# Sketched attention and a two-expert router on one core: due times of one batch's loads, the place of the last query sketches, and three steps moved between engines

## The chip, the cores and the metric

The program runs on one core of a Trainium2 chip. The metric is the device time of one execution in microseconds (us). The core has five engines that run at the same time, each through its own list of instructions in order: TensorE (PE; its weight loads are listed as PEld), VectorE (DVE), ScalarE (ACT), GpSimd (POOL) and SyncE (SP). SP here only issues DMA transfers; ACT and POOL issue some as well.

## The reference, cut to what matters

Four batches of four heads, 1088 tokens of 32 values each. `phi` is a feature map: two small projections (`S1`, `S2`, 8 rows each) and the outer product of their results, 64 features a token.

```python
q_p, k_p = phi(q), phi(k)
kv  = einsum('bhsf,bhsd->bhfd', k_p, v)
z   = sum(k_p, axis=2)
x   = (q_p @ kv) / (q_p . z + 1e-6)        # heads joined: (4352, 128)
logits = x @ w_gate + log1p(exp(x @ w_noise)) * noise
# the two largest of 8 logits choose two experts, softmax over the two
out = sum over the two of  weight * relu(x @ w1[e]) @ w2[e]     # 128 -> 1024 -> 128
```

## The kernel before, in words

**Stages.** For each batch, keys and queries are turned so that a token's values lie on the partitions (DVE, `turned`, L585 and L587), sketched by products with the two projections (`features`: PE L601, then a copy `lo` L319, a sum `ab` L608 and a product `phk` or `phq` L622), and the values are copied into `vaug` (ACT, L319 and L639). PE sums keys times values (L659) into `kvp`; two copies `kvT`, a product with the gate weights (`fold`, L680) and two copies `kvw` make the small matrix from which `queries` gets numerators, denominators and gate logits: PE turns `phq` (L704), a copy `pT`, PE L715, then on DVE `den` (L744, L745), `lh` and `lg`. `router` turns logits into the two experts, the gates and each token's row in its expert's list, and POOL sends the rows to DRAM by indirect DMA (`xs`, L796), one instruction for 128 rows. The tokens are routed in five waves: wave 0 is tiles 0 to 3 of batch 0, wave 1 is the rest of batch 0, waves 2 to 4 are batches 1 to 3.

**Expert blocks.** `block` takes 128 or 256 rows of one expert: `bT` (the rows, turned), PE L1081 with `w1`, a relu `h` (L1089, on ACT), PE L1096 with `w2` into `acc`, a copy `y`, and an indirect DMA of `y` to `pairs`. There are 48 blocks, with 4 + 4 + 8 products of 128 columns for each 128 rows, every product two records in the trace. The first four blocks (`DIRECT`) don't wait for rows in DRAM: a one-hot matrix `o` (L1026, four pieces of 128x128, on DVE) picks the rows out of `x` on PE (L1032, into `turn`). Blocks 4 to 7 fetch their rows through POOL; the later ones through SP, and DVE turns those (`bT<-xb`, L1071).

**What sets the order.** Nothing is ordered by the hardware at run time except by waits. A planner (`Plan`) takes jobs with an engine or a choice of engines (`EV` is ACT or DVE), a cost, a priority (lower goes first) and dependencies, and simulates the engines: of the jobs that can start within 0.3 us of the earliest one it takes the one of the lowest priority number. The order that comes out is each engine's list of instructions. A load's end is planned from its size at 320 GB/s, one transfer after the other, plus a `margin`; the margin is not a wait on the chip, it only tells the planner from when on a job that reads the data may be put into an engine's list. Where PE would be idle before 28 us of planned time, `idle` fills the gap with products of zeros (L1401, into `hp`), as many as fit the planned gap, some of them tied to steps of the router.

**Names that the change touches.** `load_kq` and `load_v` load keys, queries and values (SP; for batch 0, values by SP and ACT in turn); all copies L639 and L319 of batch 1's `vaug` are ACT's. `constants` has the load of ACT's function table (L511, priority 3; the first value loads have priority 1 and are issued by ACT too). `kvT` is one tile, its two halves copied by ACT or DVE as the plan has it. `rest_of_queries` sketches the last five query tiles of batch 0 (one of 64 tokens, four of 128); before, both pieces wait for the gather of block 0 and write a `bank`. In wave 0 of `router`, POOL makes `a` (L856), `row` (L857) and their sum (L858), and then three steps on `sp` (L861 to L863); DVE's `noisy` (L875) waits for these. After it on DVE come `top`, `pick`, `first`, `mk`, `gm`, `pos` and block 0's `o`.

**Buffers.** Of `bank` there are 3 in PSUM, of `acc`, `hp` 2 and of `turn` 1; of `vld` 1 and of `kq` 2.

Of the kernel before, what the change touches and what calls it, by code (L numbers as in the profile page):

```python
# [13 lines left out]
ALU = mybir.AluOpType  # L14
# [23 lines left out]
class Plan:  # L38
# [17 lines left out]
    def new(self, tag):  # L56
        return Buf(tag)
# [117 lines left out]
def kernel(  # L175
# [15 lines left out]
    P = nc.NUM_PARTITIONS  # L191
    B, H, S, DH = q.shape
    R = S1.shape[0]
# [9 lines left out]
    C = 8  # L203
    HB = 64
    YW = DH + 1 + 2 * E
# [22 lines left out]
    V, A, G, T, Y = nc.vector, nc.scalar, nc.gpsimd, nc.tensor, nc.sync  # L228
# [4 lines left out]
    def add(engines, cost, emit, **kw):  # L233

        if hold and engines in ("DVE", "PE"):
            kw["after"] = tuple(kw.get("after", ())) + tuple(hold)
        elif hold and engines == EV:
            engines = "ACT"
        return plan.add(engines, cost, emit, **kw)
# [3 lines left out]
    def tag(name, bufs, shape, dtype=F32, space=pool):  # L243
        plan.tag(name, bufs, lambda: space.tile(list(shape), dtype, name=name, tag=name, bufs=bufs))
# [16 lines left out]
    tag("qT", 1, [P, S])  # L261
    tag("lo", 2, [P, 4, 2 * R * H])
    tag("ab", 2, [P, 4 * H, 2, R])
    tag("kvT", 1, [P, 2, 2, R * R])
    tag("pT", 2, [P, 512])
    tag("den", 2, [P, 2 * H])
    tag("lh", 2, [P, 2 * H, 2 * E])
# [25 lines left out]
    def vec(n):  # L293
        return 0.155 + 0.00104 * n

    def act(n):
        return 0.155 + 0.00086 * n
# [7 lines left out]
    def mm(n):  # L305
        return max(0.205, 0.016 + 0.00162 * n)
# [6 lines left out]
    def either(n):  # L313
        return {"ACT": act(n), "DVE": vec(n)}
# [3 lines left out]
    def copy(e, o, i):  # L318
        paces.append(A.copy(o, i) if e == "ACT" else V.tensor_copy(o, i))  # L319
# [32 lines left out]
    def load_kq(b, which, prio):  # L352
        t = new("kq")
        {"k": klds, "q": qlds}[which][b] = t
        src = {"k": k, "q": q}[which]
        dma("SP", lambda: t.t[:], lambda: pairs_of(src[b]), (), [t], prio, size=557e3,
                  margin=MARGIN if b > 1 else 1.0 if b else QLATE if which == "q" else KLATE)

    def load_v(b, prio, queues=("SP",)):
        t = new("vld")  # L360
        vlds[b] = t
        src = v[b].rearrange("h (t n) d -> t h n d", n=TN)
        for l in range(4):
            dma(queues[l % len(queues)], lambda l=l: t.t[32 * l:32 * l + 32, :, 0:C, :].rearrange("p h c d -> p h (c d)"),
                lambda l=l: src[:, :, C * l:C * l + C, :].rearrange("t h c d -> t h (c d)"),
                (), [(t, l)], prio, size=131e3, issue=1.2, margin=MARGIN if b > 1 else 1.0 if b else VLATE)
        for l in range(2):
            dma(queues[l % len(queues)], lambda l=l: t.t[32 * l:32 * l + 32, :, C, :], lambda l=l: src[:, :, 32 + l, :],
                (), [(t, 4 + l)], prio, size=16e3, issue=0.6)

    w1s = const.tile([P, E, F], F32, name="w1s")
    w2s = const.tile([P, E, FJ, D], F32, name="w2s")
# [62 lines left out]
    def constants():  # L435
# [72 lines left out]
        add("DVE", 0.3, lambda e: (V.tensor_copy(starts[:, 0, :], base[:]), V.memset(over[:], -1.0)),  # L508
            r=["base"], w=[("starts", 0), "over"], prio=45)

        add("ACT", TABLE, lambda e: A.preload_act_table_set("natural_log_exp_and_others"), w=["tables"], prio=3)  # L511

    began = []

# [73 lines left out]
                            s[:, 0:P * C].rearrange("p (l c d) -> p c l d", l=4, d=DH)[:, c0:c1, :, :])  # L588
        add("DVE", vec(128 * (c1 - c0) if c0 < C else 64), emit, r=[src], w=[(dst, t) for t in range(c0, c1)], prio=prio)

    def features(jobs, prio, after=(), first=None):

        ps = new("bank")
        n = len(jobs)
        rows = slice(0, HB if jobs[0][1] == C else P)
        W = 2 * R * H

        def emit(e):
            for i, (xT, t, _) in enumerate(jobs):
                lhsT = xT.t[:, P * t:min(P * t + P, S)]  # L600
                T.matmul(ps.t[rows, 2 * W * i:2 * W * i + 2 * W], lhsT=lhsT,  # L601
                         rhs=sk[:].rearrange("p c h x -> p (c h x)"), start=True, stop=True)
        last = add("PE", n * mm(128), emit, lat=0.15, r=["sk"] + [(xT, t) for xT, t, _ in jobs],
                   w=[ps], prio=prio if first is None else first, touch=[dst for _, _, dst in jobs], after=after)
        lo, ab = new("lo"), new("ab")
        x4 = lambda: ps.t[rows, 0:2 * W * n].rearrange("p (i c y) -> p i c y", i=n, c=2)
        add(EV, either(W * n), lambda e: copy(e, lo.t[rows, 0:n, :], x4()[:, :, 1, :]), r=[ps], w=[lo], prio=prio)
        add("DVE", vec(W * n), lambda e: V.tensor_tensor(  # L608
            out=ab.t[rows, 0:n * H, :, :].rearrange("p (i h) w r -> p i (h w r)", h=H),
            in0=x4()[:, :, 0, :], in1=lo.t[rows, 0:n, :], op=ALU.add), r=[ps, lo], w=[ab], prio=prio)  # L610

        def factors(i, m, w):
            return ab.t[rows, H * i:H * m, w, :]
        i = 0
        while i < n:
            m = i
            while m < n and m - i < 2 and jobs[m][2] is jobs[i][2]:
                m += 1

            def product(e, i=i, m=m):  # L620
                shape = [rows.stop, H * (m - i), R, R]
                V.tensor_tensor(  # L622
                    out=jobs[i][2].t[rows, jobs[i][1]:jobs[m - 1][1] + 1, :, :].rearrange("p c h (i j) -> p (c h) i j", i=R),
                    in0=factors(i, m, 0).unsqueeze(3).to_broadcast(shape),
                    in1=factors(i, m, 1).unsqueeze(2).to_broadcast(shape), op=ALU.mult)
            add("DVE", vec(256 * (m - i)), product, r=[ab], w=[(jobs[i][2], jobs[x][1]) for x in range(i, m)], prio=prio)
            i = m
        return last
# [4 lines left out]
    def keys_values(b, prio, head=False, after=()):  # L633
# [19 lines left out]
        for ts in ((0, 1), (2, 3), (4, 5), (6, 7), (8,)) if head else (range(C + 1),):  # L653
            def emit(e, ts=ts):
# [6 lines left out]
                                 start=(t == 0 and a == 0), stop=(t == C), skip_group_check=True)  # L661
            add("PE", 2 * len(ts) * mm(P), emit, lat=0.15, w=[kvp], prio=prio + 3.5,
                r=[(pk, t) for t in ts] + [(va, h) for h in range(H + (C in ts))])
        kvT, kvw = new("kvT"), new("kvw")
        kv_of[b] = (kvw, pq)

        def rows_of(l):
            return slice(64 * l, 64 * l + DH + 1)

        for l in range(2):  # L670
            add(EV, either(128), lambda e, l=l: copy(
                e, kvT.t[rows_of(l), l, :, :],
                kvp.t[rows_of(l), 0:2 * P].rearrange("p (a f) -> p a f", a=2)[:, :, 64 * l:64 * l + 64]),
                r=[kvp], w=[(kvT, l)], prio=prio + 3)
        ps = new("bank")

        def fold(e):
            for l in range(2):
                for a in range(2):
                    T.matmul(ps.t[64 * l:64 * l + 64, YW * a:YW * a + YW], lhsT=kvT.t[rows_of(l), l, a, :],  # L680
                             rhs=wg4[rows_of(l), a, :], start=True, stop=True)
        folded = add("PE", 0.46, fold, lat=0.15, r=[kvT, "wg"], w=[ps], prio=prio + 3)
        for l in range(2):
            add(EV, either(98), lambda e, l=l: copy(
                e, kvw.t[64 * l:64 * l + 64, :, YW * l:YW * l + YW],
# [1 line left out]
                r=[ps, "kvw0"], w=[(kvw, l)], prio=prio + 3)  # L687
        turned(qT, qld, 4, 8, prio + 5)
        if head:
            return lambda: (behind_first.extend((features([(qT, C, pq)], prio + 26, (), 913), features([(qT, t, pq) for t in range(4, 8)], prio + 26, (), 914)))), folded  # L690
        features([(qT, t, pq) for t in range(4, 8)], prio + 6, after)

    def queries(b, t0, t1, prio):
# [109 lines left out]
    def router(b, t0, n, w, x, lg, prio):  # L803
# [4 lines left out]
        def t3(name):  # L808
            return B_[name].t[:, 0:n, :]
# [4 lines left out]
        def z():  # L814
            return lg.t[:, 0:n, E:2 * E]
# [38 lines left out]

        def large_on_pool(e):
            G.tensor_scalar(out=t3("a"), in0=z(), scalar1=EXP_MAX, scalar2=1e37, op0=ALU.is_gt, op1=ALU.mult)  # L856
            G.tensor_scalar(out=t3("row"), in0=z(), scalar1=0.0, scalar2=None, op0=ALU.max)  # L857
            G.tensor_tensor(out=t3("a"), in0=t3("a"), in1=t3("row"), op=ALU.add)  # L858

        def most_of_it(e):  # L860
# [8 lines left out]

        if w == 0:  # L870

            add("POOL", 0.75, large_on_pool, r=[lg], w=[B_["a"], B_["row"]], prio=prio)
            add("POOL", 0.75, most_of_it, r=[B_["a"], B_["sp"], "noise", lg], w=[B_["sp"]], prio=prio)
            dve(5 * q1 + 0.15, rest_of_it, ["u", "noise"], ["c", "up"])
            dve(q1, lambda: V.tensor_sub(out=t3("noisy"), in0=t3("sp"), in1=t3("c")), ["sp", "c"], ["noisy"])  # L875
        else:
            dve(2 * q1, large_part, [lg], ["a"])
            dve(5 * q1, small_part, ["u", "a"], ["c", "up", "a"])
            dve(3 * q1, noisy_part, ["sp", "a", "noise", lg], ["noisy", "sp"])
# [137 lines left out]
    def block(u, w, e, r, n):  # L1017
# [5 lines left out]
        if u < DIRECT:  # L1023
            oh = new("o")
            for c in range(4):
                add("DVE", vec(64), lambda _, c=c: V.tensor_scalar(  # L1026
                    out=oh.t[:, c, :], in0=place[:], scalar1=onehot["pos"].t[:, c, e:e + 1],
                    scalar2=onehot["gm"].t[:, c, e:e + 1], op0=ALU.is_equal, op1=ALU.mult),
                    r=["place", onehot["pos"], onehot["gm"]], w=[(oh, c)], prio=-900 if u == 0 else 12 + u)
# [304 lines left out]
    load_small()  # L1334
    constants()
    decode_job()
    rest_of_queries, folded = keys_values(0, 0, head=True)
    load_kq(1, "k", 40)
    load_w(0, 41)
    for r in (0, P):  # L1340
# [13 lines left out]
    first_index(15)  # L1354
    hold.append(picked)
    keys_values(1, 100)
    rest_of_queries()
    x, lg, last = queries(0, 4, C + 1, 27)
    router(0, 4, C + 1 - 4, 1, x, lg, 30)
    for b in range(1, B):  # L1360
# [10 lines left out]
    u = 0  # L1371
# [69 lines left out]
```

## Time and profile before

| | |
|---|---|
| median of 3 runs | 355.24 us (354.42 to 355.94) |
| the profiled execution | 356.38 us, of which its span is 354.3 us |
| mean granted TensorE clock | 0.989 |
| busy: PE, DVE, ACT, POOL | 96%, 42%, 38%, 65% |
| DMA | 41.17 MB, 116 GB/s over the span |

Each line of a profile view has start and length in us, or a group's busy time and count, and in brackets the idle time of the engine just before, with what ended it. A fp32 product is two records on PE; in a steady stretch a group of 8 records takes 0.89 us. In the profile's slices a digit is the busy share of one fortieth of the span (8.86 us) in tenths; the row PEclk is the granted clock in tenths of full speed.

### The profile page before, as it was taken

The numbers are of one execution on the slowest core, as the hardware profiler recorded it, in microseconds if no ns is written. First come the engines' busy times: TensorE is split into PE (matmuls) and PEld (weight loads), VectorE is DVE, ScalarE is ACT, GpSimd is POOL, SyncE is SP. The second block draws the span as 40 slices with busy tenths as digits, with TensorE's granted clock in tenths as the row PEclk, the third lists the DMA queues.
The fourth block names the chain that finished last, engine by engine and source line by source line (L and its number), as shares of the span: only waits on it lengthen the run. The fifth ranks groups of instructions, "written<-read, shape, count | busy, mean of one in ns | idle before, by whom it ended". The sixth has DMA issues, their size and how long they took to land.

```text
span 354.3 us, 7491 instructions
## 1 busy us (share of the span) xinstructions
PE 340.8 (96%) x2593; PEld 316.4 (89%) x2595; DVE 149.0 (42%) x553; ACT 132.9 (38%) x296; POOL 232.0 (65%) x384
## 2 busy tenths in 40 slices
PE   8986999999999999999999999999999999999992
PEld 3845999999999998889999999999999999999991
DVE  6876788468976788287600000011012000001401
ACT  2342434336334343134333343334333433434330
POOL 7756647994689889888989898954533453344410
PEclk9999899999999999999999999999999999999997
DMA  7999949922361144611432223563114311114421
GB/s 197 304 365 219 325 126 370 302 65 62 81 184 48 39 75 77 149 44 37 83 72 54 58 46 63 123 170 50 37 37 144 99 32 30 29 26 146 148 94 38
DMA packets 68298, 41.17 MB, mean 116 GB/s; under 512 B 49301, under 2 KB 60438, under 8 KB 68256
## 3 DMA queue, kind: packets, MB, share of 16 engines
q1 hardware_dynamic: 62784, 30.92, 34.8%
q0 software_dynamic: 4736, 9.19, 8.2%
q10 hardware_dynamic: 736, 0.54, 0.6%
q8 instruction: 21, 0.34, 0.4%
q14 instruction: 21, 0.17, 0.2%
HBM read 24.17 MB, written 16.65 MB: 115 GB/s over the span
## 4 chain that ended last, share of the span: by engine, by line
PE 93%; DMA 2%; SPq 1%; DVE 1%; ACT 1%; issue 0%; POOL 0%; ACTq 0%; DVEq 0%
PE acc L1096 37%; PE hp L1081 35%; PE bank L601 5%; PE bank L715 4%; PE bank L659 4%; PE bank L704 2%; DMA vld<-in_v_dram 2%; PE hp L1401 1%; PE acc L659 1%; SPq L335 1%; PE bank L1228 1%; PE turn L1032 1%; PE bank L680 0%; PE bank L924 0%; DVE lg L734 0%
## 5 line engine op out<-in xcount | busy, mean ns | idle before, releaser
L1096 PEld LDWEIGHTS acc<-w2s,h 128*128 128x128 f32 x1152 | 146.9, 193 | 8.3 <-ACT h L1089 3.4
L1096 PE MATMUL acc<-w2s,h 128*128 128x128 f32 x1152 | 151.1, 276 | 3.2 <-ACT h L1089 3.2
L1081 PE MATMUL hp<-bT,w1s 128*128 128x128 f32 (+1 forms) x768 | 148.5, 329 | 0.0
L1089 ACT ACTIVATE h<-hp 128x512 f32<-128x512 f32 x144 | 85.9, 597 | 128.5 <-PE hp L1081 102.2
L1081 PEld LDWEIGHTS hp<-bT,w1s 128*128 128x128 f32 x768 | 112.4, 193 | 5.4 <-issue 0.3
L796 POOL DMA_INDIRECT pairs<-y,ix x62 | 61.3, 989 | 69.9 <-ACT y L319 58.2
L796 POOL DMA_INDIRECT xs<-xg,to x72 | 72.1, 1002 | 14.9 <-issue 10.1
L1071 DVE STREAM_TRANSPOSE bT<-xb 128x256 f32<-128x256 f32 (+1 forms) x40 | 15.5, 388 | 123.6 <-PE hp L1081 97.3
L795 POOL MEMSET zb<- 128x400 bf16 (+1 forms) x142 | 63.4, 446 | 1.3 <-PE hp L1401 1.1
L319 ACT COPY y<-acc 128x128 f32<-128x128 f32 (+1 forms) x48 | 15.3, 319 | 28.0 <-PE acc L1096 23.2
L715 PE MATMUL bank<-kvw,pT 128*128 128x98 f32 x144 | 18.6, 275 | 0.4 <-ACT pT L319 0.2
L715 PEld LDWEIGHTS bank<-kvw,pT 128*128 128x128 f32 x144 | 17.3, 192 | 1.4 <-issue 1.0
L1152 DVE TENSOR_TENSOR o<-pr 128x512 f32<-128x512 f32 (+2 forms) x13 | 6.8, 526 | 27.9 <-DMA pr<-pairs 27.9
L1401 PE MATMUL hp<-zb 128*128 128x512 bf16 x37 | 11.3, 441 | 2.5 <-DVE zb L436 1.3
L659 PE MATMUL bank<-phk,vaug 128*128 128x128 f32 (+1 forms) x108 | 13.1, 277 | 0.0
L659 PEld LDWEIGHTS bank<-phk,vaug 128*128 128x128 f32 (+1 forms) x108 | 12.5, 191 | 0.4
L622 DVE TENSOR_TENSOR phk<-ab 128x512 f32<-128x512 f32 (+1 forms) x20 | 12.3, 635 | 0.4
L622 DVE TENSOR_TENSOR phq<-ab 128x512 f32<-128x512 f32 (+1 forms) x20 | 12.2, 638 | 0.4
L319 ACT COPY pT<-bank 128x512 f32<-128x512 f32 (+1 forms) x17 | 9.1, 549 | 8.4 <-PE bank L704 4.4
L319 ACT COPY lo<-bank 128x256 f32<-128x256 f32 (+3 forms) x21 | 7.0, 335 | 11.8 <-PE bank L601 7.2
L973 DVE TENSOR_TENSOR xg<-x,g 128x512 f32<-128x512 f32 (+1 forms) x16 | 11.2, 743 | 0.0
L601 PE MATMUL bank<-sk,kT 128*128 128x128 f32 (+1 forms) x72 | 10.6, 284 | 0.3 <-DVE kT L587 0.3
(171 smaller groups left out, 244.4 us busy)
## 6 DMA issues: line engine op xcount, KB each, us to landing
xs<-pad SPq DMA_DIRECT2D x9, 516.0 KB
w1s<-in_moe_w_dram SPq DMA_DIRECT2D x8, 512.0 KB
w2s<-in_moe_w_dram SPq DMA_DIRECT2D x8, 512.0 KB
pr<-pairs SPq DMA_DIRECT2D x7, 512.0 KB
xb<-xs SPq DMA_DIRECT2D x96, 32.0 KB
kq<-in_k_dram SPq DMA_DIRECT2D x4, 544.0 KB
kq<-in_q_dram SPq DMA_DIRECT2D x4, 544.0 KB
vld<-in_v_dram SPq DMA_DIRECT2D x14, 128.0 KB
```

The source lines that it names most:

```text
L319: paces.append(A.copy(o, i) if e == "ACT" else V.tensor_copy(o, i))
L601: T.matmul(ps.t[rows, 2 * W * i:2 * W * i + 2 * W], lhsT=lhsT, rhs=sk[:].rearrange("p c h x -> p (c h x)"), start=True, stop=True)
L622: V.tensor_tensor(out=jobs[i][2].t[rows, jobs[i][1]:jobs[m - 1][1] + 1, :, :].rearrange("p c h (i j) -> p (c h) i j", i=R), in0=factors(i, ...
L659: T.matmul(kvp.t[:, P * a:P * a + P], lhsT=va.t[0:K, t, hs, :].rearrange("p h d -> p (h d)"), rhs=pk.t[0:K, t, hs, :].rearrange("p h f -> ...
L715: T.matmul(ps2.t[:, c0:c0 + 2 * YW], lhsT=pT.t[:, P * (2 * i + a):P * (2 * i + a) + P], rhs=kvw.t[:, a, :], start=True, stop=True)
L795: G.memset(zb[:, 0:FIRST_SPACER if kind == "first" else SPACER], 0.0)
L796: ins = G.indirect_dma_start(**kw)
L1071: add("DVE", vec(P * n), lambda _: V.transpose(bT.t[:, 0:P * n], flat()), r=[xb], w=[bT], prio=TOP + u)
L1081: T.matmul(hp.t[:, P * n * i:P * n * (i + 1)], lhsT=w1s[:, e, P * (js * g + i):P * (js * g + i + 1)], rhs=bT.t[:, 0:P * n], start=True, st ...
L1089: paces.append(A.activation(out=h.t[:], in_=hp.t[:], func=AF.Relu))
L1096: T.matmul(acc.t[:, D * c:D * c + D], lhsT=h.t[:, P * (n * i + c):P * (n * i + c + 1)], rhs=w2s[:, e, j, :], start=(j == 0 and c == 0), st ...
L1401: ins = T.matmul(warm()[:], lhsT=zb[:, 0:P], rhs=zb[:], start=True, stop=True)
```

## The change

It makes these edits:

1. The planned margin of batch 1's loads: keys 1.0 to 1.6 us, queries 1.0 to 6.0, values 1.0 to 8.0; the two small value pieces, 0 before, get 8.0 for batch 1 and 6.0 for batches 2 and 3.
2. The function table's load goes from priority 3 to 0, ahead of ACT's first value loads.
3. The sketch of query tiles 4 to 7 of batch 0: its PE products come behind the numerators of tiles 0 to 3, and they write an `acc` in place of a `bank`; its copy `lo` also waits for `pos` and `gm`.
4. `kvT` becomes two tiles; for batch 0 both are copied by ACT.
5. In wave 0 `row` is made by DVE in place of POOL.
6. Of block 0's four one-hot pieces POOL makes two.

```diff
-    tag("kvT", 1, [P, 2, 2, R * R])
+    tag("kvT", 2, [P, 2, R * R])
...
 def load_kq(b, which, prio):
-                  margin=MARGIN if b > 1 else 1.0 if b else QLATE if which == "q" else KLATE)
+                  margin=MARGIN if b > 1 or b and which == "q" else QLATE if which == "q" else KLATE)
 def load_v(b, prio, queues=("SP",)):
         for l in range(4):
-                (), [(t, l)], prio, size=131e3, issue=1.2, margin=MARGIN if b > 1 else 1.0 if b else VLATE)
+                (), [(t, l)], prio, size=131e3, issue=1.2, margin=MARGIN if b > 1 else 8.0 if b else VLATE)
         for l in range(2):
-                (), [(t, 4 + l)], prio, size=16e3, issue=0.6)
+                (), [(t, 4 + l)], prio, size=16e3, issue=0.6, margin=MARGIN if b > 1 else 8.0 if b else 0.0)
...
-        add("ACT", TABLE, lambda e: A.preload_act_table_set("natural_log_exp_and_others"), w=["tables"], prio=3)
+        add("ACT", TABLE, lambda e: A.preload_act_table_set("natural_log_exp_and_others"), w=["tables"], prio=0)
...
-    def features(jobs, prio, after=(), first=None):
+    def features(jobs, prio, after=(), first=None, early=None):
-        ps = new("bank")
+        ps = new("bank" if early is None else "acc")
...
-        last = add("PE", n * mm(128), emit, ..., prio=prio if first is None else first, ..., after=after)
+        last = (add if early is None else plan.add)("PE", n * mm(128), emit, ...,
+                   prio=prio if first is None else first, ..., after=after if early is None else (early,))
+        gone = [] if early is None else [onehot["pos"], onehot["gm"]]
-        add(EV, either(W * n), lambda e: copy(e, lo.t[rows, 0:n, :], x4()[:, :, 1, :]), r=[ps], w=[lo], prio=prio)
+        add(EV, either(W * n), lambda e: copy(e, lo.t[rows, 0:n, :], x4()[:, :, 1, :]), r=[ps] + gone, w=[lo], prio=prio)
...
         for l in range(2):
-            add(EV, either(128), lambda e, l=l: copy(
-                e, kvT.t[rows_of(l), l, :, :],
+            add("ACT" if head else EV, act(128) if head else either(128), lambda e, l=l: copy(
+                e, kvTs[l].t[rows_of(l), :, :],
...
-            return lambda: (behind_first.extend((features([(qT, C, pq)], prio + 26, (), 913), features([(qT, t, pq) for t in range(4, 8)], prio + 26, (), 914)))), folded
+            def rest(early):
+                behind_first.append(features([(qT, C, pq)], prio + 26, (), 913))
+                features([(qT, t, pq) for t in range(4, 8)], prio + 26, (), prio + 11, early)
+            return rest
...
         def large_on_pool(e):
             G.tensor_scalar(out=t3("a"), in0=z(), scalar1=EXP_MAX, scalar2=1e37, op0=ALU.is_gt, op1=ALU.mult)
-            G.tensor_scalar(out=t3("row"), in0=z(), scalar1=0.0, scalar2=None, op0=ALU.max)
             G.tensor_tensor(out=t3("a"), in0=t3("a"), in1=t3("row"), op=ALU.add)
...
-            add("POOL", 0.75, large_on_pool, r=[lg], w=[B_["a"], B_["row"]], prio=prio)
-            add("POOL", 0.75, most_of_it, r=[B_["a"], B_["sp"], "noise", lg], w=[B_["sp"]], prio=prio)
+            dve(q1, lambda: V.tensor_scalar_max(t3("row"), z(), 0.0), [lg], ["row"])
+            add("POOL", 0.6, large_on_pool, r=[lg, B_["row"]], w=[B_["a"]], prio=prio)
+            add("POOL", 1.0, most_of_it, r=[B_["a"], B_["sp"], "noise", lg], w=[B_["sp"]], prio=prio)
...
             for c in range(4):
-                add("DVE", vec(64), lambda _, c=c: V.tensor_scalar(
+                add(("POOL" if u == 0 and c % 2 else "DVE"), 0.3 if u == 0 and c % 2 else vec(64), lambda e_, c=c: (
+                    G if e_ == "POOL" else V).tensor_scalar(
                     out=oh.t[:, c, :], in0=place[:], scalar1=onehot["pos"].t[:, c, e:e + 1],
                     scalar2=onehot["gm"].t[:, c, e:e + 1], op0=ALU.is_equal, op1=ALU.mult),
...
-    rest_of_queries, folded = keys_values(0, 0, head=True)
+    rest_of_queries = keys_values(0, 0, head=True)
...
-    rest_of_queries()
+    rest_of_queries(last)
```

More of the change, by code (lines that the diff above doesn't have):

```diff
@@ L602, in emit @@
                          rhs=sk[:].rearrange("p c h x -> p (c h x)"), start=True, stop=True)
-        last = add("PE", n * mm(128), emit, lat=0.15, r=["sk"] + [(xT, t) for xT, t, _ in jobs],
-                   w=[ps], prio=prio if first is None else first, touch=[dst for _, _, dst in jobs], after=after)
+        last = (add if early is None else plan.add)("PE", n * mm(128), emit, lat=0.15, r=["sk"] + [(xT, t) for xT, t, _ in jobs],
+                   w=[ps], prio=prio if first is None else first, touch=[dst for _, _, dst in jobs], after=after if early is None else (early,))
         lo, ab = new("lo"), new("ab")
+        gone = [] if early is None else [onehot["pos"], onehot["gm"]]
         x4 = lambda: ps.t[rows, 0:2 * W * n].rearrange("p (i c y) -> p i c y", i=n, c=2)
-        add(EV, either(W * n), lambda e: copy(e, lo.t[rows, 0:n, :], x4()[:, :, 1, :]), r=[ps], w=[lo], prio=prio)
+        add(EV, either(W * n), lambda e: copy(e, lo.t[rows, 0:n, :], x4()[:, :, 1, :]), r=[ps] + gone, w=[lo], prio=prio)
         add("DVE", vec(W * n), lambda e: V.tensor_tensor(
@@ L663, in keys_values @@
                 r=[(pk, t) for t in ts] + [(va, h) for h in range(H + (C in ts))])
-        kvT, kvw = new("kvT"), new("kvw")
+        kvTs, kvw = (new("kvT"), new("kvT")), new("kvw")
         kv_of[b] = (kvw, pq)
@@ L670, in keys_values @@
         for l in range(2):
-            add(EV, either(128), lambda e, l=l: copy(
-                e, kvT.t[rows_of(l), l, :, :],
+            add("ACT" if head else EV, act(128) if head else either(128), lambda e, l=l: copy(
+                e, kvTs[l].t[rows_of(l), :, :],
                 kvp.t[rows_of(l), 0:2 * P].rearrange("p (a f) -> p a f", a=2)[:, :, 64 * l:64 * l + 64]),
-                r=[kvp], w=[(kvT, l)], prio=prio + 3)
+                r=[kvp], w=[kvTs[l]], prio=prio + 3)
         ps = new("bank")
@@ L679, in fold @@
                 for a in range(2):
-                    T.matmul(ps.t[64 * l:64 * l + 64, YW * a:YW * a + YW], lhsT=kvT.t[rows_of(l), l, a, :],
+                    T.matmul(ps.t[64 * l:64 * l + 64, YW * a:YW * a + YW], lhsT=kvTs[l].t[rows_of(l), a, :],
                              rhs=wg4[rows_of(l), a, :], start=True, stop=True)
-        folded = add("PE", 0.46, fold, lat=0.15, r=[kvT, "wg"], w=[ps], prio=prio + 3)
+        folded = add("PE", 0.46, fold, lat=0.15, r=[*kvTs, "wg"], w=[ps], prio=prio + 3)
         for l in range(2):
```

## The prediction

> **What bounds the kernel now.** I read the page first: busy shares and slices.
>
> ```profile
> PE 340.8 (96%) x2593; PEld 316.4 (89%) x2595; DVE 149.0 (42%) x553; ACT 132.9 (38%) x296; POOL 232.0 (65%) x384
> ...
> PEclk9999899999999999999999999999999999999997
> ```
>
> PE is the bound almost everywhere, so only two things save time: an idle PE, and PE work that moves into a stretch where PE has nothing real to do. One inner slice, the fifth (35.4 to 44.3 us), has a lower clock. Next, the waits of PE alone:
>
> ```profile
> PE acc L1096 <- ACT h L1089: 3.2, 1, 3.2
> PE hp L1401 <- DVE zb L436: 1.3, 1, 1.3
> ```
>
> There is one large wait on an engine that is otherwise full: block 0's second product waits 3.2 us for a relu on ACT. (The other is the start.) What the relu waits for, the chain in order of time says, and ACT's timeline beside it:
>
> ```profile
> 25.81 8.17 DMA vld<-in_v_dram
> ...
> 34.89 1.16 PE acc L1096 x8
> 36.05 0.58 PE turn L1032 x4
> 36.63 1.71 PE acc L1096 x8
> 38.34 2.47 PE hp L1081 x16
> ```
>
> ```profile
> 29.50 0.37 ACT L319 COPY lo<-bank 128x256 f32<-128x256 f32 x1 [0.88 <-PE bank L601]
> 34.05 0.30 ACT L639 COPY vaug<-vld 64x128 f32<-64x128 f32 x1 [4.17 <-DMA vld<-in_v_dram]
> 34.25 1.07 ACT L1089 ACTIVATE h<-hp 128x512 f32<-128x512 f32 x2
> 35.22 1.32 ACT L319 COPY vaug<-vld 128x256 f32<-128x256 f32 x4
> ```
>
> In ACT's list the small copy of batch 1's values stands ahead of block 0's relus; its data lands at 33.97, and two relus whose products were complete by about 31.3 wait behind it. The `vaug` of batch 1 itself is first read by PE at 63.0 (first record of L659 there): nobody needs it early. Last, the windows, for the clock after the wait:
>
> ```profile
> 36.00:37.00 1.00, 1.00 (x8) 1.00 (x7) 0.33 (x2) 0.54 (x2) 0.97 (x2) 0.61 1.10 376
> 37.00:38.00 1.00, 1.00 (x7) 1.00 (x6) 1.00 (x5) 0.00 (x0) 0.83 (x2) 0.50 1.01 353
> 38.00:39.00 1.00, 1.00 (x7) 1.00 (x7) 0.94 (x4) 0.27 (x1) 0.83 (x3) 0.50 1.09 350
> 39.00:40.00 1.00, 1.00 (x8) 1.00 (x8) 0.97 (x3) 0.05 (x1) 1.00 (x2) 0.68 1.12 390
> ```
>
> After the busy times of the five engines comes the granted clock (0.61, 0.50, 0.50, 0.68): after the idle stretch PE runs at half speed for some 3.4 us. From 40 us on PE is never idle for long again until the tail.
>
> **The change part by part.** The sum is made against the profiled execution, 356.38 us with a span of 354.3; it lies 1.14 above the median, and I take the gain off the median.
>
> *Margins of batch 1's values.* The loads issued up to and with these values add up to 8.17 MB by the sizes in the code (five of keys, queries or values with 0.56 each, noise 0.14, four experts' weights 4.19, two clears 1.06); at the planner's 320 GB/s that ends at about 27 us, so their copies were planned from about 28 (small pieces) and 29 (large). Block 0's relus come out just behind, and on the chip the data came 5 us later than planned. With 8.0 the copies are planned from about 36, two us behind the true landing, and block 0's relus, which wait for nothing else by then, go ahead of them. Gain: 3.2 of idle PE, and the lost clock, 0.39 + 0.50 + 0.50 + 0.32 = 1.7. What is late next: the gather of block 1 (o pieces of DVE, 30.05 to 31.2) and its `bT`, both due before 32; weights 1 to 3 were issued by 19.7. The copies now stand ahead of later relus, 1.6 us of ACT work in all, on an engine busy 38%. The other margins (queries of batch 1, used at 59.8; small pieces of batches 2 and 3, on which ACT never waited) I cost at nothing: a longer planned wait for data that is not used for 20 us. If that cover is gone, the price is the second rival's.
>
> *Sketch of tiles 4 to 7.* On the path now, between block 0's gather and its first product:
>
> ```profile
> 27.95 1.52 PE L601 MATMUL bank<-sk,qT 128*64 128x128 f32 x10
> 29.30 1.95 PE L1081 MATMUL hp<-bT,w1s 128*128 128x128 f32 x16
> ```
>
> Eight of the ten records go to about 19.7, where PE runs filling products. Two stay, and ACT's copy of `bT` (28.05 to 28.32) lies beside them, so L1081 can start at 28.35 to 28.4 rather than 29.30: gain 0.9. The copy `lo` stays behind `pos` and `gm` (26.2), when ACT is idle (2.02 us before 28.05): nothing. Its sum and two products (0.4 + 1.3 on DVE) come after the one-hot pieces, as now; new is that block 1's `acc` is the buffer that this sum must have read. DVE has about 1.5 us for that before block 1's L1096, some 5.5 us after block 0's first product; nothing, or 0.4 if a one-hot piece stands ahead.
>
> *`row` by DVE.* GpSimd's steps, which end the wait before `noisy`:
>
> ```profile
> 21.66 0.31 POOL L857 TENSOR_SCALAR row<-lg 128x32 f32<-128x32 f32 x1
> ...
> 23.57 0.19 DVE L875 TENSOR_TENSOR noisy<-sp,c 128x32 f32<-128x32 f32 x1 [0.53 <-POOL sp L863]
> ```
>
> POOL's sum then starts at 21.66 instead of 22.05: 0.39 less, and DVE's wait of 0.53 takes it. On DVE the step (0.2) fits into the 0.29 before L841, which waits for ACT. The planner now thinks these POOL steps longer, though, and may fill PE with one or two products of 0.22 too many ahead of the counts (L921, ready for 0.2 us already). I take 0.3.
>
> *One-hot pieces.* DVE's four take 1.12 us, 0.26 apart. No row has this form on POOL. Below: a cast of 128x128 there took 0.29, so two end 0.66 after `pos` and, with 0.27 from a POOL end to its reader (23.30 to 23.57), the gather is done 0.3 sooner. Above: L856 over 128x32 took 0.34 and L929 over 128x4 0.25, 3.3 ns an element; 128 make 0.66, two 1.4, and the gather is 0.5 later. I take 0.42 (L856 and 96 elements at the cast's slope): no gain, no loss. VectorE saves 0.5 that is not on the path. The Trainium skill (GPSIMD Engine Reference, 3.1) speaks against this step: elementwise work belongs on VectorE, GpSimd taking about twice as long, 2.6 cycles an element to 1 for two inputs. By that, as an estimate, twice DVE's 0.26 to 0.34 would make the gather 0.1 to 0.5 later; the trace's own rows reach from one side to the other.
>
> *`kvT` by ACT.* Already serial: DVE's half starts (15.78) when ACT's has ended (15.75). Both by ACT end about 0.1 sooner, but the fold's first product (15.92) is not held by the second half. The planned gap grows by a copy, so one more filling product of 0.22 may precede the fold: loss 0.1.
>
> *Function table first.* It takes 1.28 us (2.79 to 4.07) and now stands ahead of ACT's three value loads (1.46 to 2.76). If the issues wait for the engine, they are 1.28 later. The copies of batch 0's values, 8.29 to 10.09, waited for these loads, and PE waited 0.1 us at 10.14 for the last copy, with PE full from there to 15.45: up to 1.3 us lost. If not, nothing: at 34.19 ACT's queue already worked on the wait of a later copy, while L639 (34.05 to 34.35) ran, so the queue goes past a busy engine. I take nothing, and keep 1.3 as the other end. A gain is excluded: ACT idles 4.2 us before 8.29 anyway. The Trainium skill (ScalarE: Activation LUTs, What ACT_TABLE_LOAD costs) adds a drain of 1.38 us to a load; this trace shows none; with it, as an estimate, up to 2.7 rather than 1.3 would be lost.
>
> *Sum:* 3.2 + 1.7 + 0.9 + 0.3 - 0.1 = 6.0; 355.24 - 6.0 = 349.2. A little goes to waits that the old stall hid (below), 0.2: **349.4**.
>
> **The rivals.**
>
> *It doesn't do what it says* (same). Where the copies land in ACT's list comes out of a simulation. If they still precede block 0's relus, the wait ends at 33.97 as now, and the 1.1 us won ahead of it are only waited longer: 355. For: the planner misjudged this landing by 5 us. Against: 7 us more than cover that.
>
> *The rows of wave 2 come too late* (slower). After 40 us the tightest spot is block 16, the first of wave 2: DVE's transpose waits for `xb` until 130.42 and PE starts on it at 132.48, a slack of 1.6. With PE 6 us earlier, POOL's sends must move too, and they hang on batch 1's keys and queries, whose loads are just the ones planned later. If the sends keep their times, PE idles some 4 us there, and with 1.7 of clock all is lost: that is the point where it decides. Each us beyond costs one; if batch 1's part falls back by 2 to 4 us, 357.5 to 360. For: GpSimd is 90% busy or more from 98 to 232. Against: just before 98 it still waits for PE and ACT (gaps of 2.2, 1.5, 2.4), so it follows them.
>
> *The table delays the values* (faster, less): 0.5 to 1.3 lost, or small new waits of that sum after 28 us: 350.5.
>
> **How the numbers follow.** Forecast 0.54 (348.2 to 350), table or small waits 0.23 (350 to 352.5), unchanged 0.11, slower rival 0.12. What can be told from no change is about 0.5%, 1.8 us. Faster: 0.54 + 0.23 + 0.02 of the mixed cases = 0.79; same 0.10, slower 0.11. Low: 349.4 with the one-hot's 0.3, the rest of `row`'s 0.1 and `lo`'s cover holding, and some run-to-run spread: 348.0. High: up to the unchanged case, 355.0, since 0.77 without it is too little. The likeliest case's own range is 348.2 to 350.
>
> **What would show it.** Right: no PE wait for `h` near 31, granted clock 1.0 through 36 to 40, ACT's `vaug` copies of batch 1 behind the relus of block 0 and with no DMA wait, L601 x8 at 19.7, L1081 first at about 28.2, `noisy` at 23.2. Wrong: ACT idle until 34 again; a wait of PE on `bT` near 125; copies of batch 0's values starting after 9.

## The result, and the profile after

The changed kernel takes 354.39 us (median of 22 runs, 351.72 to 356.69), the kernel before 354.45 (22 runs beside them, 352.29 to 356.53): a ratio of the means of 1.001, with an interval of 0.999 to 1.003. There is no difference that can be measured. The profiled execution of the changed kernel took 353.93 us with a span of 351.8. Line numbers are those of the kernel that is shown, in the changed kernel up to 6 higher than before and in the experiments' kernels up to 13 higher.

First the page: busy shares, the slices of PE, and the granted clock.

```profile
PE 339.7 (97%) x2589; PEld 316.5 (90%) x2590; DVE 145.7 (41%) x547; ACT 134.5 (38%) x301; POOL 232.6 (66%) x385
...
PE   8999999979999999999999999999999999999992
...
PEclk9999999989999999999999999999999999999997
```

The dent of the clock has gone from the fifth slice and stands in the ninth (70 to 79 us), where PE's own row has a 7. The waits of PE say what it is:

```profile
PE hp L1087 <- DVE bT L1077: 2.5, 1, 2.5
...
PE bank L926 <- DVE mk L919: 0.6, 1, 0.6
```

The wait of 3.2 us for a relu is gone, and a new one of 2.5 stands for a transpose of VectorE. In ACT's timeline the forecast order is to be seen: block 0's relus (`h`) first, and behind them batch 1's copies, with no DMA in the brackets. (The small copy L641 follows at 39.02.)

```profile
29.32 0.60 ACT L1095 ACTIVATE h<-hp 128x512 f32<-128x512 f32 x1 [0.94 <-PE hp L1087]
...
36.04 0.41 ACT L319 COPY vaug<-vld 128x256 f32<-128x256 f32 x1
...
37.40 1.02 ACT L319 COPY vaug<-vld 128x256 f32<-128x256 f32 x3
```

And the place where the time went again, in the chain in order of time and in the timeline of all engines:

```profile
65.93 0.90 POOL xs L801
...
67.45 5.26 DMA pairs<-y,first_at
...
73.98 1.76 DMA xb<-xs
```

```profile
72.68 1.74 SPq L335 DMA_DIRECT2D xb<-xs  x4
...
75.83 0.31 DVE L1077 STREAM_TRANSPOSE bT<-xb 128x128 f32<-128x128 f32 x1 [3.65 <-DMA xb<-xs]
...
76.29 1.35 PE L1087 MATMUL hp<-bT,w1s 128*128 128x128 f32 x8 [2.47 <-DVE bT L1077]
```

Block 8 is the first that SP fetches. Its rows are those of wave 1, which POOL sends to DRAM in ten instructions. In the kernel before these ran from 57.08 to 72.73, SP's fetch came at 74.79, 2.06 us after the last, and DVE reached the transpose at 78.36 without a wait. Now POOL sends from 51.69 to 66.83, 5.4 to 5.9 us earlier, as much as PE is ahead (block 4's transpose on PE at 49.61 for 55.00 before). But the fetch starts at 72.68, 5.85 us after the last send: the rows are only 2.1 earlier. The row "5.26 DMA" is that time. (The chain names `pairs<-y,first_at`, which POOL issues on the same queue; SP's own wait is listed as one for `xs<-xg,to`.) The windows of before and of after say what the landing keeps to (the last two columns are the DMA share and GB/s):

```profile
70.00:72.00 2.00, 2.00 (x21) 2.00 (x20) 0.17 (x1) 1.20 (x2) 1.66 (x4) 1.00 0.83 202
72.00:74.00 2.00, 2.00 (x20) 2.00 (x20) 1.82 (x8) 0.75 (x2) 1.83 (x3) 1.00 0.20 48
```

```profile
68.00:70.00 2.00, 2.00 (x21) 2.00 (x20) 1.79 (x9) 0.85 (x2) 1.83 (x3) 1.00 0.98 246
70.00:72.00 2.00, 2.00 (x21) 2.00 (x20) 1.54 (x6) 0.04 (x1) 0.06 (x1) 1.00 0.46 132
```

The DMA engines are full until about 72 us before and until about 70 to 71 after. Ahead of the rows are SP's loads of two experts' weights, batch 2's keys, queries and values, and five clears of the buffer, issued from 47.39 us on (49.17 before). That traffic moved by 1.8 us, and the rows with it, by 2.1. DVE takes its list in order and stands 3.65 us at the transpose; behind it are the product `x` and the router's steps, and PE has done what else it has. Then the clock, in the windows (the granted clock stands behind the busy times of the five engines):

```profile
76.00:77.00 1.00, 0.71 (x6) 0.74 (x7) 0.97 (x6) 0.27 (x1) 0.83 (x3) 1.00 0.36 64
77.00:78.00 1.00, 1.00 (x7) 1.00 (x6) 1.00 (x2) 0.32 (x1) 0.60 (x1) 0.52 0.14 1
78.00:79.00 1.00, 1.00 (x7) 1.00 (x6) 0.93 (x4) 1.00 (x4) 0.00 (x0) 0.50 0.41 93
79.00:80.00 1.00, 1.00 (x7) 1.00 (x7) 0.83 (x4) 0.02 (x1) 0.00 (x0) 0.50 0.24 46
80.00:81.00 1.00, 1.00 (x8) 1.00 (x8) 0.90 (x9) 0.13 (x1) 0.00 (x0) 0.77 0.13 17
```

0.48 + 0.50 + 0.50 + 0.23 = 1.71 us are lost here, so the new stall costs 2.47 + 1.71 = 4.2 us in this execution; in the profile before the old one cost 3.19 + 1.7 = 4.9.

### The profile page after: what moved, and what is told of

Read it like the earlier page. It is cut to its first block, busy times and chain, and to the rows that moved or that the text cites. A ratio compares the mean times of both kernels' runs of the same rounds, so it can differ in the third digit from the quotient of the medians.

```text
span 351.8 us, 7486 instructions
## 1 busy us (share of the span) xinstructions
PE 339.7 (97%) x2589; PEld 316.5 (90%) x2590; DVE 145.7 (41%) x547; ACT 134.5 (38%) x301; POOL 232.6 (66%) x385
## 4 chain that ended last, share of the span: by engine, by line
PE 87%; POOL 5%; DMA 2%; DVE 2%; issue 1%; ACT 0%; SPq 0%; POOLq 0%; DVEq 0%; ACTq 0%
PE acc L1102 35%; PE hp L1087 35%; PE bank L602 5%; PE bank L720 3%; POOL xs L801 3%; PE bank L661 2%; PE bank L709 2%; DMA pairs<-y,first_at 1%; PE hp L1407 1%; POOL zb L800 1%; PE acc L661 1%; PE turn L1038 1%; PE bank L1234 1%; DMA xb<-xs 1%; PE bank L682 0%
## 5 line engine op out<-in xcount | busy, mean ns | idle before, releaser
L319 ACT COPY pT<-bank 128x512 f32<-128x512 f32 (+1 forms) x19 | 10.2, 541 | 8.1 <-PE bank L709 7.3
L709 PE MATMUL bank<-ident,phq 128*128 128x128 f32 x72 | 11.2, 279 | 0.0
```

Of the source, the lines that this page charges most:

```text
L709: T.transpose(ps.t[:, c0:c0 + P], pq.t[:, t + i, 2 * a:2 * a + 2, :].rearrange("p h f -> p (h f)"), ident[:])
```

## The experiments

Three theories. **A:** the gains at the head are real, and they are lost at block 8, because its rows land with the DMA traffic of 48 to 72 us and not with POOL's sends, and because DVE stands at the transpose with other work behind it. **B:** the other edits lose what the margins gain. **C:** GpSimd's and the rows' pace bounds the stretch, whatever the order. Each run is compared with runs of the kernel before beside it (medians 354.98, 354.50 and 354.44 in the three groups, four kernels each).

### e1_margins and e2_all_but_margins: the first edit alone, and all but it

```diff
# e1: the kernel before, with this alone; e2: the changed kernel, with this undone
-   margin=MARGIN if b > 1 else 1.0 if b else ...        (load_kq; load_v the same)
+   margin=MARGIN if b > 1 or b and which == "q" else QLATE if which == "q" else KLATE   (load_kq)
+   margin=MARGIN if b > 1 else 8.0 if b else VLATE      (load_v, large pieces)
+   margin=MARGIN if b > 1 else 8.0 if b else 0.0        (load_v, small pieces)
```

> Only edit 1 (the planned margins of batch 1's loads), on the kernel before. Theory A (PE gets ahead, and then block 8 has to wait for the rows of wave 1, whose scatters are held up by the loads and clears that go out behind the first fetch, 48 to 72 us): PE's wait near 31 is gone, a wait of PE for block 8's bT of 1 to 2.5 us appears near 76, and the time stays within 0.5% of before (353 to 356). Theory B (the margins are worth the forecast 5 us, and the other edits, the one-hot pieces on GpSimd above all, lose it again): no wait near 76, about 349.5.

> Edits 2 to 6 without edit 1, on the kernel after. Theory A: ACT stands before batch 1's values again and PE waits near 31, some 1 us longer than before because PE is there earlier and the landing is not; no wait near 76; the time within 0.5% of before (353.5 to 355.5). Theory B: slower than before by 3 us or more.

Measured: e1 354.51 us, ratio 0.998 (0.996 to 1.001); e2 355.52, ratio 1.000 (0.997 to 1.003). In e1 the wait near 31 is gone, and one of 3.02 has come at 80 (DVE and PE, timeline of e1):

```profile
79.74 0.31 DVE L1071 STREAM_TRANSPOSE bT<-xb 128x128 f32<-128x128 f32 x1 [4.62 <-DMA xb<-xs]
79.98 0.25 DVE L319 COPY bT<-turn 128x128 f32<-128x128 f32 x1
...
80.29 1.01 PE L1081 MATMUL hp<-bT,w1s 128*128 128x128 f32 x3 [3.02 <-DVE bT L319]
```

Here PE doesn't even wait for block 8: it waits for the copy of a block in front of it, which stands behind block 8's transpose in DVE's list. So the first edit alone takes the old wait away and gets the new one; B is not needed for the loss. (The wait is larger than A's 1 to 2.5 us.) In e2 both of A's waits were missed: the old one near 31 was expected back and did not come, since with edits 2 to 6 alone the plan already puts the relus first, and one came at 76 where none was expected. There ACT stood 5.41 us at batch 2's small copy (75.44), whose data came late, and PE waited 4.13. It is the first edit that gives these small pieces their margin; the prediction put that part at nothing, and once the head is earlier it isn't nothing. So each half removes the first wait by itself, and neither has kept the gain.

### e3_late_clears and e4_before_late_clears: less traffic in front of the rows

```diff
...
-        later(lambda r=r: clear(r, 60 + r / P))
+        if r < 6 * P:
+            later(lambda r=r: clear(r, 60 + r / P))
+        else:
+            late_clears.append(clear(r, 60 + r / P))     # depends on block 8's fetch of xb
...
```

> The kernel after, with the last three clears of the row lists (1.58 MB; needed by waves 3 and 4 only) put behind block 8's fetch in the list of SP. Theory A: between 48 and 72 us there is a quarter less traffic, the last scatter of wave 1 lands 2 to 3 us after its issue instead of 5.7, PE's wait near 76 is gone or under 1 us, and the time is about 350.5 (349.5 to 351.5). Theory C (the wait comes from the pace of GpSimd's ten sends, 1.6 us each, and not from the DMA engines): the landing stays near 72, the wait of 2.5 us stays, about 354.4.

> The same three clears put late in the kernel before, which keeps its wait near 31. Theory A: the rows of wave 1 land earlier, but nobody waited for them, so the time is as before (353.5 to 355.5). If the clears' traffic itself cost PE time in another way, this would be faster by as much as the run of the kernel after with late clears.

Measured: e3 356.12 us, ratio 1.002 (0.999 to 1.005); e4 364.04, ratio 1.024 (1.019 to 1.029). In e3 the last send ends at 68.98 and the fetch starts 1.4 us later, for 5.85 in the changed kernel; the wait at 76 is gone. SP, POOL in e3's timeline:

```profile
68.08 0.90 POOL L801 DMA_INDIRECT xs<-xg,to  x1 [0.18 <-issue]
...
70.39 1.74 SPq L335 DMA_DIRECT2D xb<-xs  x4
```

The DMA share over 50 to 72 us is 0.82 there and 0.97 in the changed kernel. The last send ends 2.1 us later than in the changed kernel, and yet the fetch starts 2.3 us earlier. With less traffic ahead the rows land sooner, whatever the sends do: the traffic is the cause of the late landing. The time is not better, since two of the clears, 0.5 MB each, were put at 74.57 on SP, and the next block's fetch behind them came at 79.62: DVE stands 5.04 us at 84.89, PE waits 3.54 at 86.72. In e4 the same edit in the kernel before kept the old wait (3.07) and made three of 1.9 to 2.5 us from 91 to 142; that its time would be the same was wrong. A transfer that is put off must also be put somewhere.

### f1_row_margin and f4_before_row_margin: a due time for the rows

```diff
-                        there, [(xb, l)], -10 + u, size=16e3 * n, issue=0.5, done=done)
+                        there, [(xb, l)], -10 + u, size=16e3 * n, issue=0.5, done=done,
+                        margin=4.0 if u < 12 else 0.0)
```

The same edit in the changed kernel (f1) and in the kernel before (f4).

> The changed kernel in which the plan takes SyncE's fetches of blocks 8 to 11 (`xb`, the rows of wave 1) as 4 us late; no instruction is added or left out, only their order may change. Theory A (the gain of the head is lost at 76 us because VectorE, in order, stands 3.65 us at block 8's transposes until the rows land, while other work for TensorE lies behind them): VectorE's copies of batch 1's last tile and of block 7 come ahead of block 8's transposes, the wait of 2.47 us at 76 and the half clock behind it (4.3 us together) shrink to under 1.5 us, and the span is 2 to 3 us shorter, 349 to 352 us. Theory C (the rows set the pace of the whole queue of blocks, whatever the order): the wait comes at another place, at 78 to 90, with about the same size, and the time stays within 0.5% of before. Theory B (the other edits lose the gain elsewhere): the wait goes and the time stays.

> The kernel before, with the planned lateness of 4 us on the fetches of blocks 8 to 11 alone (the control for f1_row_margin). Theory A: before has no wait for rows at 76, so nothing is to be gained there; the wait of 2.96 us near 31 and the half clock behind it stay, and the time is within 0.3% of before. Theory M (the margin is worth 3 to 4 us by itself, and the change nothing): 350.5 to 351.5 us, as f1_row_margin.

Measured: f1 350.73 us (350.03 to 351.22), ratio 0.990 (0.987 to 0.993); f4 353.83, ratio 0.997 (0.994 to 0.999). With the margin alone the time falls by 0.6 us, with the change alone by 0.1, with both by 3.8: with the rows' due time right, the change is worth 3.1 us (353.83 - 350.73), and M, by which the margin would be worth 3 to 4 us by itself and the change nothing, falls. C expected the wait elsewhere with its old size; it is at 80 with 1.60, for a relu that stands in VectorE's list behind block 8's transpose. The windows of f1 and the clock:

```profile
78.00:80.00 2.00, 0.48 (x5) 0.29 (x3) 1.47 (x12) 0.60 (x1) 1.83 (x3) 1.00 0.24 34
80.00:81.00 1.00, 0.92 (x8) 0.92 (x9) 1.00 (x17) 0.21 (x1) 0.54 (x2) 1.00 0.41 94
```

PE loses 1.6 us and then has the full clock: the half clock of 1.7 us, which followed the wait of 2.47, is not there. (A's "under 1.5 us" was missed by 0.1.) f4 has the old wait for a relu, in its profiled run 2.24 us (3.19 in the profile before), and 1.7 us of half clock behind it.

### f2_row_margin_dve_onehots and e6_dve_onehots: the sixth edit undone

```diff
-   add(("POOL" if u == 0 and c % 2 else "DVE"), 0.3 if u == 0 and c % 2 else vec(64), ...   # o
+   add("DVE", vec(64), ...
```

> The kernel f1_row_margin with all four of block 0's one-hot rows on VectorE again. GpSimd's two took 0.87 and 0.80 us in the trace of the changed kernel, where VectorE's take about 0.26: the gather's last product and the first product of h start 0.5 to 0.9 us earlier (27.3 to 27.6 in place of 28.12). Theory A: the time is shorter than that of f1_row_margin by as much, 0.5 to 0.9 us. Theory C: h starts earlier and the wait for rows grows by as much; the same time.

> The changed kernel with all four of block 0's one-hot rows on VectorE again, and nothing else altered. Every theory: the first product of h starts 0.5 to 0.9 us earlier than the 28.12 of the changed kernel. A and C: the wait at 76 us grows by about as much, since the rows' landing does not move, and the time is the same within 0.3%. B: the time is 0.5 to 0.9 us shorter.

Measured: e6 355.20 us, ratio 1.003 (1.000 to 1.005); f2 351.50, ratio 0.992 (0.989 to 0.994). The first product of `h` starts at 27.71 in e6 (28.12 in the changed kernel) and at 27.60 in f2 (28.32 in f1): the two pieces on GpSimd cost 0.4 to 0.7 us of the head. Neither kernel is faster for it. In e6 the wait at 76 has grown to 4.27 us (at 78); its plan also sends wave 1 later (52.92 for 51.69). In f2 PE waits 1.73 at 80 and 0.68 at 122. B and A's "shorter by as much" for f2 are both missed. In e6 the wait grew by 1.8 us, more than the 0.4 that was won, and the half clock behind it lasts 6.83 us. In f2 the wait at 80 is 0.1 longer, and the one at 122 is for `mk`, not for rows; the two would take back the 0.7 that was won. That f2's median is 0.8 above f1's stays open.

### f3_spread_clears, f7_row_margin_spread_clears, f6_margins_row_margin, f8_row_margin_7us

```diff
# f3: the changed kernel;  f7: f1_row_margin   (the list late_clears is filled as in e3)
...
+                if u in (12, 14, 16):
+                    late_clears.pop(0).deps.add(fetch)      # one clear behind each fetch
# f6: e1_margins with the margin of f1;  f8: f1 with 7.0 for 4.0
```

> The changed kernel in which three of SyncE's clears of the buffer (rows 6P, 7P and 8P; 0.5 MB each) are planned one each behind the fetches of blocks 12, 14 and 16, where e3_late_clears had all three behind block 8's. Theory A: as there, the rows of block 8 land 1 to 2 us behind the last send of their wave and the wait at 76 us is gone; block 9's fetch is no longer behind two clears, so that the wait of 3.5 us at 86 is gone too, and the span is 2 to 4 us shorter, 348 to 352 us. If the transfers that are put off only collide with the rows of wave 2 instead, a wait of 1 to 3 us comes between 95 and 130 us and the time is the same.

> f1_row_margin and f3_spread_clears together: planned lateness of 4 us on the fetches of blocks 8 to 11, and three clears one each behind the fetches of blocks 12, 14 and 16. Theory A: the rows of block 8 land 2 to 4 us earlier and the order leaves them time as well, so the wait of 1.60 us that f1_row_margin has left at 80 is gone; 348.5 to 350 us, the fastest. If the put-off clears hold up later rows, a wait of 1 to 3 us comes at 85 to 130 and the time is 350 to 353.

> The kernel before with the change's margins on batch 1's values and queries (the first part alone) and the planned lateness of 4 us on the fetches of blocks 8 to 11. Theory A: the wait near 31 and its half clock are gone (4.9 us of the forecast), the wait of 3.02 us that e1_margins had at 80 shrinks below 1.8; 350 to 352 us. By the difference to f1_row_margin the other five edits are worth 0.5 to 1.2 us, the earlier head; if they are worth nothing, the two have the same time.

> f1_row_margin with a planned lateness of 7 us in place of 4. Theory A: TensorE is given more other work ahead of block 8; the wait of 1.60 us at 80 is gone, unless other work in that stretch is used up, in which case wave 1's blocks are moved into a later gap; 349 to 351 us. If rows set the pace (theory C), the same time as f1_row_margin or more, with the wait at a later block.

Measured: f3 352.12 us, ratio 0.993 (0.990 to 0.996); f7 350.19 (350.03 to 350.61), ratio 0.989 (0.987 to 0.991), the fastest of all; f6 353.20, ratio 0.997 (0.996 to 0.999); f8 353.25, ratio 0.997 (0.996 to 0.999).

f3's time is at the slow end of what A said, and its way only in part A's: two of the clears went to 94 us and one to 142 without a new wait there, but the two others of that stretch stayed at 53, the fetch still came 4.0 us after the last send, and PE waits 2.92 at 78. f7, with both edits, has no large wait left: PE's list of waits and the clock's row of its page:

```profile
PE hp L1414 <- DVE zb L436: 1.3, 1, 1.3
PE bank L926 <- DVE mk L919: 0.5, 1, 0.5
PE bank L1238 <- ACT y L319: 0.4, 1, 0.4
```

```profile
PEclk9999999999999999999999999999999999999997
```

Its median, just above A's 348.5 to 350, is 4.3 below that of before. That its span, 348.3, lies 6.0 below the 354.3 of the profile before, the sum that was forecast, is in part luck: the profiled execution of before was a long one, and f7 has two edits more than the change. f6 and f8 both missed A's figures. f6 has the first wait removed and the rows' margin but not the other five edits: it is 2.5 us slower than f1. Of that, 1.0 is the earlier head (first product of `h` at 29.34 and 28.32), and 1.0 is that two waits of 1.00 and 1.62 at 86 and 97 stand for the 1.60 in f1; the other 0.5 stays open. In f8 seven microseconds were too many: 2.5 us more than f1. Two waits of 1.1 us, at 85 and 93, stand there for one of 1.6; that explains 0.6 of the 2.5, and the rest stays open. Of the three due times that were tried, 0, 4 and 7 us, the middle one is the best.

## Why the prediction was wrong, and where it was right

The forecast was a clear gain; there is none, and the measured time stands within the range only because the range reached to the unchanged case.

**The step that failed** is the last: "From 40 us on PE is never idle for long again until the tail", and in the sum 0.2 us for "waits that the old stall hid". That 0.2 was 4.2: 2.47 of idle PE at 76 and 1.71 of half clock. It takes for granted that the rest moves with PE by 6 us. The sends did, the rows did not.

**The second rival had the mechanism, at another place.** It let DVE wait for rows and named the price, "PE idles some 4 us there, and with 1.7 of clock all is lost". It looked at wave 2, since the slack of PE is smallest at block 16, 1.6 us; there nothing happened (no wait near 125). But VectorE, in order, stands at a transpose also when PE has other work, and then holds up what lies behind. By VectorE's list block 8's rows were early by only some 0.5 us in the kernel before, as an estimate: the last of their four fetches is issued about 76.1 and takes 1.76 us to land, as in the changed kernel, which is 77.9, and VectorE took them at 78.36. Nor was this landing read against the one thing that moves little, the DMA traffic ahead of the rows. And the rival's condition, sends that keep their times, did not hold: the sends moved by 5.4 to 5.9 us, the landing by 2.1. (Its support, GpSimd busy for 90% or more from 98 to 232, is 88% by the windows.) One row of before would have told, with a DMA share of 1.00 over the time of the ten sends:

```profile
50.00:72.00 22.00, 22.00 (x201) 21.23 (x200) 14.73 (x53) 8.67 (x23) 16.63 (x25) 1.00 1.00 319
```

**Margins** (3.2 + 1.7): right in mechanism; the clock is 1.00 through 36 to 40. The size is that of one execution, though: f4's profile has 2.24 + 1.7 for the same stall, and the profiled run of before was 1.9 us above the median of 22. Nor is the half clock there in every execution, it seems: the profiled runs without one ahead of the tail have a mean granted clock of 0.993 or more, those with one stretch of it 0.988 to 0.990, and of the 75 runs of the kernel before that lie beside the experiments 27 have 0.993 or more. So, as an estimate, about a third of its executions had no 1.7 to win. e2 shows that the first edit isn't the only way to it. And with the rows' due time right, the first edit alone is worth 0.6 us (353.83 in f4 to 353.20 in f6), the other five on top of it 2.5 (to 350.73 in f1): the large term of the sum isn't the large part of the gain that f1 has.

**Head** (0.9 + 0.3 - 0.1 = 1.1): the total came, 29.30 to 28.12, by other terms. `noisy` starts at 22.68, 0.9 earlier for the 0.3 of the `row` term. About half is there before the router, since the numerators start at 17.30 for 17.82: `kvT` was costed at a loss of 0.1. The sketch (L602 x8 at 19.16) went as forecast, and the one-hot pieces took back 0.4 to 0.7:

```profile
L1032 POOL TENSOR_SCALAR o<-place,pos,gm 128x128 f32<-128x128 f32 x2 | 1.7, 836 | 0.8 <-DVE pos L947 0.8
```

836 ns each, where 0.42 was taken and 0.66 was the upper bound. The nearest rows had no scalar operand for each partition, or fewer elements; this form, with two operands a partition, takes 2.5 times what DVE's two pieces beside it take (0.66 us for both). The Trainium skill (GPSIMD Engine Reference, 3.1) speaks of about twice; it spoke against the step, rightly, and the ratio here is larger.

**Function table** (0): right; the third rival did not come. It loads while ACT's queue issues the three value loads, and batch 0's copies start at 8.34 for 8.29:

```profile
1.46 1.28 ACT L511 ACT_TABLE_LOAD   x1 [1.46 <-PEq L1430]
1.49 1.30 ACTq L335 DMA_DIRECT2D vld<-in_v_dram  x3
```

**What stays open.** The stall sums give 4.9 + 1.2 - 4.2 = 1.9 us of gain in the profiled runs (their spans differ by 2.5), and about 0.9 with f4's 2.24; the medians show 0.1. The runs of the changed kernel spread over 5 us with mean granted clocks from 0.983 to 0.997, those of f1 over 1.2 with 0.993 to 0.997. The number of stretches at half clock fits that: the profiled run of the changed kernel, with one, has 0.988, and e2's and e6's, with one of twice the length, 0.984 to 0.986; of the changed kernel's 22 runs three have 0.996 or more (352.7 us in the mean) and five 0.983 or 0.984 (356.3). But only one execution of each kernel was profiled, so this is not shown. Nor is it settled how the traffic holds the rows back: the runs show that the clears do (e3); the weights' loads were not moved, and by which rule the DMA engines share their time no run tells.

## What to carry to other kernels

A stall that is removed moves everything behind it forward, except what hangs on transfers: before such a gain is booked to the end, find the first data fetched from DRAM that each in-order engine reads behind it, and ask whether its landing moves too or is fixed by the traffic in front of it. Where the order is planned, a late datum needs its lateness in the plan, each one that becomes the latest in turn; too much of it can cost nearly as much as too little (f8). A wait that is left is best kept short: in the profiled runs those of 1.60 to 1.73 us cost their own length, and most of those from 1.89 up the clock as well.

## What the runs showed of the hardware

- **Idle time and the half clock.** In the traces the half clock comes in stretches of 3.41 us (77.04 to 80.45 in the changed kernel) or two or three times that (6.83 in e2 and e6, 10.24 in e4), and each 3.41 us cost 1.7. It followed waits of PE of 1.89 (e4), 2.24 (f4), 2.47 (the changed kernel), 2.92 (f3) and 3.02 us (e1). Waits of 1.60 (f1), 1.62 (f6) and 1.73 us (f2) left the clock at 1.00, but so did one of 2.54 in e4 (at 142.06), so the length of a wait doesn't decide alone. Nor does PE's busy time in the 3.41 us ahead: in e4 it is 1.52 in two such windows, and the half clock follows the first and not the second. What else counts is open.

```profile
88.97:92.38 3.41, 1.52 (x12) 1.16 (x12) 3.14 (x18) 1.21 (x4) 2.22 (x5) 1.00 0.96 264
92.38:95.79 3.41, 2.61 (x13) 2.34 (x13) 0.13 (x1) 0.27 (x1) 0.00 (x0) 0.50 0.80 144
...
140.17:143.58 3.41, 1.52 (x7) 1.40 (x8) 2.01 (x8) 0.32 (x1) 3.07 (x5) 1.00 0.54 81
143.58:147.00 3.42, 2.64 (x14) 1.49 (x13) 2.13 (x5) 1.73 (x4) 2.62 (x4) 1.00 0.69 113
```

The Trainium skill (TensorE: Matmul & The Clock Gate, HAM oscillation) gives the rule of no idle gaps over some 3.4 us; here gaps of 1.89 to 3.02 were enough, in the runs named. Its time of some 3.4 us of sustained work until the full clock (the same page, Part 1: The HAM clock gate) agrees with the 3.41.

- **Rows by GpSimd's queue behind bulk loads.** From the last send to the fetch that needs it went 5.85 us in the changed kernel, at a DMA share of 0.97 over 50 to 72 us, 4.0 at 0.87 (f3), 2.75 at 0.85 (f7) and 1.4 at 0.82 (e3). In the kernel before it was 2.06 at 1.00: its last sends came as the traffic ended. In the ten profiled kernels that keep all five clears there, the last sends end between 66.8 and 72.7 us, and the fetch starts between 72.7 and 75.5.
- **ACT's queue goes past a running table load:** 0.03 us after its start it issues the next DMA. The Trainium skill (ScalarE: Activation LUTs, What ACT_TABLE_LOAD costs) adds a drain of 1.38 us for every switch to a different set; no run here tests it, since ACT's load ends at 2.74 us and its next instruction starts only at 7.43, and in the kernel before ACT has nothing to do from 4.07 to 8.29, so that a drain would not show in either trace.
